# A strided convolution with group norm and GELU, forward and backward, on one core: 1 MB gradient stores move to GpSimd's queue, GELU's cube term becomes two instructions, two spreading copies replace three, and the order tables are written anew

## Chip, cores and metric

The kernel runs on 1 core of one Trainium2 chip. The metric is device time in microseconds (us); less is better. The time before is the median of three runs. The profile is that of one further execution.

## What is computed

```python
# x [2,16000,256], w [31,256,256], gamma, beta [256], grad_out [2,7985,256], all bf16
h = sum over i of einsum('blc,cd->bld', x[:, i:i+2*L:2, :], w[i])     # K=31, stride 2, L=7985
mu, var = mean and variance of h over l, per batch and channel
out = gelu_tanh((h - mu) / sqrt(var + 1e-5) * gamma + beta)
# returned: out, and the gradients of x, w, gamma, beta for grad_out
```

So there are three large matrix products: the convolution (forward), the gradient of `x`, and the gradient of `w`.

## The kernel before, in words

The three products are not done tap by tap. Taps are grouped by the branches A, B_ and C_, and a Karatsuba-like scheme at up to three levels replaces products by sums and differences of operands: VectorE (DVE) prepares the sums in SBUF (all large tiles are pieces of one buffer `arena`), TensorE (PE) multiplies into PSUM (`ps`, four slots of two banks in `ring`), ScalarE (ACT) and DVE combine results there.

The work has five stages, named in the code by `plan.stage`:

- **F0**, **F1**: the forward convolution of batch 0 and of batch 1. `f_sums` (L688 to L730, helper line L694) makes operand sums on DVE, `f_mm` (L736) multiplies, `f_three_b` (L756) multiplies one shared product into the first bank and then spreads it, with signs, over both banks by ACT copies (L772). In F1 the GELU of batch 0 and its derivative run beside it (`gelu_batch`, `gelu_unit`, L1086).
- **G0**, **G1**: the gradient of `x`. `input_grad` (L1411) goes over batch `b`, chunk `c` (four of them), half `pr` and branch. `e_load` (L1191) brings two spilled tensors back from DRAM (`dyd`, `hd`, 512 KB each for each `dh`), `e_comp` (L1199) combines them on DVE (L1206, L1208, L1217) and ACT spreads the result. `g_sums` (L1277) makes differences, `g_mm` (L1324) multiplies, `g_evac` (L1387) adds a PSUM pair to `GRB` into `HO`, a single buffer of 1 MB (L1395), and the fourth such addition of a half is followed by its store to `out_1` (L1399). `dl_turn` (L1254) transposes operand tiles for the next stage by DMA on SyncE's queue (SP, L549) and stores each from GpSimd's queue (POOL) to a DRAM tensor `dld` (128 KB each, 144 of them). In G0 the GELU of batch 1 runs beside it.
- **W**: the gradient of `w`, nine combinations `n` (COMBOS). `x_raw` and `d_tile` load operands on SP, `w_add` (L1496), `pair_x` (L1598), `pair_d` (L1609, L1614) and `leaf_d` (L1699) make sums on DVE, `w_mm` (L1528) multiplies, `w_pairs` (L1617) makes a shared product and spreads it by ACT copies (L1630), `w_both` (L1638), `ve` (L816) and `keep` (L831) move partial results, `w_emit` (L1550, L1557) writes finished taps and stores them.

**What sets the order.** Every operation is recorded by `Plan.add` with an engine, an estimated duration and its data. `Plan.order` gives each a due time, worked back from the position of PE's work, and shifts it by two tables in us: `lead`, by stage and function, and `fine`, by stage, function and part (chunk or `n`). `Plan.listing` then makes a list of each engine's instructions from the estimated durations and due times, and `emit` issues them in that order, which is kept. So every engine runs its instructions strictly in the listed order: an instruction that waits holds up all that stand behind it on its engine. The estimated duration of an ACT instruction of `n` elements comes from `act(n)` (L31).

`load` (L536) sends a transfer of over 4096 bytes to SP in every stage, whatever queue its caller names, unless `own=True` is passed. So the stores of `out_1` go through SP, in one row with the loads of `e_load`, the transposes and the loads of stage W; the `dld` stores pass `own=True` and go through POOL.

Of the kernel before, what the change touches and what calls it, by code (L numbers as in the profile page):

```python
# [12 lines left out]
ACT = mybir.ActivationFunctionType  # L13
# [17 lines left out]
def act(n, extra=0.0):  # L31
    return 0.06 + n * 0.00097 + extra
# [6 lines left out]
class Plan:  # L39
# [3 lines left out]
    def __init__(self, tc):  # L43
# [10 lines left out]
            "F0 f_evac last": 5.0,  # L54
            "F0 f_mm f_leaf": -288.0,
            "F0 f_mm f_outer": -149.5,
            "F0 f_mm f_three_ac": -4.5,
            "F0 f_mm f_three_b": -5.5,
            "F0 f_mm pe_turn": -527.0,
            "F0 f_outer forward": -46.0,  # L60
            "F0 f_seed forward": -48.5,
            "F0 f_three_b forward": -129.5,
            "F0 keep f_evac": 35.5,
            "F0 load conv_stem_kernel": -15.5,
            "F0 load f_evac": 42.5,
            "F0 tt f_sums": -120.5,
            "F0 tt second": 20.5,
            "F0 tt third": -36.0,
            "F0 turn w2_part": -3.0,
            "F0 turn x_load": -8.5,  # L70
            "F0 ve f_seed": -122.5,
            "F0 ve_neg f_seed": 49.0,
            "F0 w_sub f_first": -76.5,
            "F0 w_sum w2_part": -13.5,
            "F1 f_evac last": -106.5,
            "F1 f_mm f_leaf": -335.0,
            "F1 f_mm f_outer": 74.0,
            "F1 f_mm f_three_ac": -8.5,
            "F1 f_mm f_three_b": -75.5,
            "F1 f_three_b forward": -73.0,  # L80
            "F1 gelu_unit gelu_batch": -2.0,
            "F1 load gelu_unit": 23.0,
            "F1 load out0_store": 15.0,
            "F1 tt f_sums": -79.5,
            "F1 tt gelu_unit": -49.5,
            "F1 tt second": -38.0,
            "F1 tt third": -225.5,
            "F1 turn gelu_batch": 56.0,
            "F1 turn gelu_unit": -12.5,
            "F1 turn x_load": 35.5,  # L90
            "F1 w_sub f_again": 4.5,
            "G0 e_comp e_load": 0.5,
            "G0 g_evac last": 1.5,
            "G0 g_mm g_leaf": -24.5,
            "G0 g_mm g_outer": 22.0,
# [369 lines left out]
def conv_stem_kernel(  # L465
# [620 lines left out]
    def gelu_unit(b, c, e, tiles, go, oo):  # L1086
# [23 lines left out]
        def tt(o, a, b_, op):  # L1110
            add("DVE", dve(nf), [o], [a, b_], lambda: V.tensor_tensor(out=o, in0=a, in1=b_, op=op))  # L1111
# [745 lines left out]
```

## Time and profile before

| what | value |
|---|---|
| median of three runs | 1153.68 us (1152.89 to 1154.54) |
| the profiled execution's own time | 1154.13 us |
| its span, first to last instruction | 1152.4 us |
| mean granted TensorE clock | 0.994 |
| PE, DVE, ACT, POOL busy | 1122.5, 997.9, 532.7, 125.4 us |
| DMA issues of 1 MB (and two of 832 KB) from `arena` to `out_dram` on SP | 14 and 2 |

How to read it: PE is the engine that is nearly always busy, so the profile's useful questions are where PE is idle and what ended each idle stretch. DVE has little room either, but its idle time costs nothing by itself. The view of waits lists, for each engine and line, what was waited for, the total in us, how often, and the longest. The timeline gives the start, the length, the engine and line, and in brackets the idle time of that engine just before, with what ended it. A `q` behind an engine's name means its queue's sequencer: it issues DMAs or waits.

### The profile page before, as it was taken

To read this page: it belongs to the slowest core of one execution; us is meant where nothing else is said; L and a number is where in the kernel's file an instruction comes from. 1 tells how busy PE (TensorE), PEld (TensorE's weight loads), DVE (VectorE), ACT (ScalarE), POOL (GpSimd) and SP (SyncE) were. 2 spreads that over 40 slices of the span, in tenths; PEclk is the share of its full clock that TensorE was granted. 3 is DMA by queue.
4 is the path that set the end of the run, shared out by engine and by line. 5 is a ranking of instruction groups with operands and counts; after the bars stand their busy time and mean duration, and the time that the engine had idled before them with its cause. 6 is when DMAs were issued, how large, how long until landed. Compare 5 with 4: busy or idle time off the path is not lost. (4 is left out here: it accounts for less than half of the span.)

```text
span 1152.4 us, 18848 instructions
## 1 busy us (share of the span) xinstructions
PE 1122.5 (97%) x7652; PEld 749.9 (65%) x7652; DVE 997.9 (87%) x920; ACT 532.7 (46%) x817; POOL 125.4 (11%) x221
## 2 busy tenths in 40 slices
PE   5999999999999999999999899999999999999998
PEld 3888899877777874444444344444588666656785
DVE  7997787798989997999999787877799998689995
ACT  1354444768776588897744355722211212211200
POOL 0000000000000012232323223232100000000000
PEclk8999999999999999999999999999999999999999
DMA  9476657769795599999888779787997825899484
GB/s 219 69 189 119 167 156 150 171 173 203 189 232 129 203 370 267 278 274 270 225 213 189 154 203 214 201 218 147 297 293 225 305 88 167 303 296 371 146 254 119
DMA packets 345807, 243.57 MB, mean 211 GB/s; under 512 B 233377, under 2 KB 316967, under 8 KB 341543
## 3 DMA queue, kind: packets, MB, share of 16 engines
q1 hardware_dynamic: 338615, 223.47, 72.5%
q0 software_dynamic: 7104, 18.89, 5.9%
q8 instruction: 60, 0.98, 0.4%
q14 instruction: 28, 0.23, 0.1%
HBM read 106.24 MB, written 80.25 MB: 162 GB/s over the span
## 5 line engine op out<-in xcount | busy, mean ns | idle before, releaser
L736 PE MATMUL ps<-arena 128*128 128x256 bf16 (+4 forms) x3460 | 407.8, 281 | 12.4 <-DMA arena<-in_x_dram 5.5
L1324 PE MATMUL ps<-arena 128*128 128x512 bf16 x1872 | 404.5, 377 | 6.9 <-DVE arena L1277 3.4
L736 PEld LDWEIGHTS <-arena 128*128 128x128 bf16 x3460 | 338.9, 99 | 81.0 <-DMA arena<-in_x_dram 5.7
L1324 PEld LDWEIGHTS <-arena 128*128 128x128 bf16 x1872 | 183.5, 98 | 226.8 <-issue 11.4
L1528 PE MATMUL ps<-arena 128*128 128x256 bf16 (+1 forms) x2320 | 311.2, 297 | 6.5 <-DVE arena L1598 4.9
L1528 PEld LDWEIGHTS <-arena 128*128 128x128 bf16 x2320 | 227.5, 98 | 90.3 <-DVE arena L1598 5.7
L831 ACT ACTIVATE arena<-ps 128x1024 f32<-128x1024 f32 x109 | 111.0, 1022 | 262.3 <-PE ps L1528 90.1
L694 DVE TENSOR_TENSOR arena<-arena 128x2080 bf16<-128x2080 bf16 (+8 forms) x126 | 156.5, 1267 | 34.0 <-PE ps L736 33.6
L544 POOL DMA_DIRECT2D dld<-arena x144 | 104.3, 727 | 261.9 <-DMA arena<-arena 248.3
L1111 DVE TENSOR_TENSOR arena<-arena 128x2048 bf16<-128x2048 bf16 (+1 forms) x80 | 95.7, 1196 | 9.6 <-ACT arena L1103 5.3
L1277 DVE TENSOR_TENSOR arena<-arena 128x1032 bf16<-128x1032 bf16 (+1 forms) x126 | 87.5, 725 | 8.7 <-ACT arena L1226 3.3
L1496 DVE TENSOR_TENSOR arena<-arena 128x4096 bf16<-128x4096 bf16 x38 | 86.2, 2286 | 7.4 <-DMA arena<-in_x_dram 3.8
L1385 DVE TENSOR_TENSOR ps<-ps,arena 128x2048 f32<-128x2048 f32 x30 | 68.9, 2296 | 26.0 <-ACT arena L831 14.8
L1395 DVE TENSOR_TENSOR arena<-ps,arena 128x1024 bf16<-128x1024 f32 x64 | 77.0, 1218 | 8.1 <-PE ps L1324 4.8
L851 ACT ACTIVATE arena<-ps 128x512 bf16<-128x512 f32 (+1 forms) x64 | 37.1, 581 | 54.0 <-PE ps L736 53.4
L1630 ACT COPY ps<-ps 128x256 f32<-128x256 f32 x54 | 19.2, 358 | 85.2 <-PE ps L1528 84.1
L553 POOL MEMSET arena<- 128x128 bf16 (+11 forms) x40 | 8.6, 245 | 425.4 <-DVE arena L694 140.0
L1351 ACT COPY ps<-ps 128x512 f32<-128x512 f32 x48 | 27.7, 578 | 46.8 <-PE ps L1324 45.6
L1699 DVE TENSOR_TENSOR arena<-arena 128x4608 bf16<-128x4608 bf16 x16 | 40.6, 2551 | 4.7 <-PE ps L1528 4.7
L806 ACT ACTIVATE arena<-ps 128x512 f32<-128x512 f32 x56 | 29.7, 597 | 32.5 <-DVE ps L816 18.8
L772 ACT ACTIVATE ps<-ps 128x256 f32<-128x256 f32 x75 | 27.6, 369 | 34.7 <-PE ps L736 33.5
L1614 DVE TENSOR_TENSOR arena<-arena 128x2048 bf16<-128x2048 bf16 x36 | 42.8, 1218 | 0.8 <-DMA out_dram<-arena 0.8
(81 smaller groups left out, 717.1 us busy)
## 6 DMA issues: line engine op xcount, KB each, us to landing
arena<-in_x_dram SPq DMA_DIRECT2D x40, 1024.0 KB
dld<-arena POOLq DMA_DIRECT2D x144, 128.0 KB, 3.9
arena<-hd SPq DMA_DIRECT2D x32, 512.0 KB
out_dram<-arena SPq DMA_DIRECT2D x14, 1024.0 KB
arena<-dld SPq DMA_DIRECT2D x18, 640.0 KB
arena<-dld SPq DMA_DIRECT2D x18, 576.0 KB
vl<-arena SPq DMA_DIRECT2D x36, 256.0 KB
arena<-vl SPq DMA_DIRECT2D x9, 1024.0 KB
```

What stands on the lines that cost most here:

```text
L544: lambda: e.dma_start(out=out, in_=in_), dma=np_ * ns / 16e3 * 1.03, ns=ns, tp=SH[pk], slack=slack)
L694: lambda: nc.vector.tensor_tensor(out=o, in0=a, in1=b, op=ALU.add))
L736: yield nc.tensor.matmul(ps[:, dh, cs], lhsT=wt, rhs=mv, start=s0, stop=False, skip_group_check=True)
L831: lambda: nc.scalar.activation(out=out, in_=ps, func=ACT.Copy, scale=scale))
L1111: add("DVE", dve(nf), [o], [a, b_], lambda: V.tensor_tensor(out=o, in0=a, in1=b_, op=op))
L1277: lambda: nc.vector.tensor_tensor(out=o, in0=a, in1=b, op=ALU.subtract))
L1324: yield nc.tensor.matmul(ps[:, e, 0:wide], lhsT=lt, rhs=mv, start=s0, stop=False, skip_group_check=True)
L1385: lambda: nc.vector.tensor_tensor(out=o, in0=x, in1=g, op=ALU.add))
L1395: lambda: nc.vector.tensor_tensor(out=ho[:, :, k, :], in0=ps[:], in1=g, op=ALU.add))
L1496: add("DVE", dve(4096), [o], [a, b], lambda: nc.vector.tensor_tensor(out=o, in0=a, in1=b, op=ALU.add))
L1528: yield nc.tensor.matmul(ps[:, s, c0:c1], lhsT=lt, rhs=mv, start=s0, stop=False, skip_group_check=True)
L1614: add("DVE", dve(2048), [o], [u, v], lambda o=o, u=u, v=v: nc.vector.tensor_tensor(out=o, in0=u, in1=v, op=ALU.subtract))
```

## The change

Five edits.

1. The store of a finished half of `out_1` passes `own=True`, so GpSimd issues it. These 16 transfers leave SP's row and stand in POOL's, among the `dld` stores.
2. In `gelu_unit`, `z = (y2 + 1/a) * y` was one scalar_tensor_tensor; it becomes a tensor_scalar (add) and a tensor_tensor (multiply), with `z` rounded to bf16 between them.
3. In `f_three_b` and `w_pairs` three ACT copies of 256 elements become one of 256 and one of 512 (the second writes two pieces by a stepped or repeated view).
4. `act(n)` is another line: 0.15 + 0.00085 n in place of 0.06 + 0.00097 n.
5. Both tables of shifts hold other numbers and partly other keys, so the lists of all engines differ from before in many places. No matrix product is added or removed.

```diff
 def act(n, extra=0.0):
-    return 0.06 + n * 0.00097 + extra
+    return 0.15 + n * 0.00085 + extra
...
-            "G1 load e_load": -8.0,
+            "G1 load e_load": -10.5,
...
-            "G1 load e_load": {0: -112.0, 1: -15.0, 2: -56.0, 3: 1.0},
+            "G1 load e_load": {0: -88.5, 1: 40.5, 3: -2.0},
...
-        for o, i, sc in ((ps[:, 1, 0:HM], ps[:, 0, HM:512], 1.0), (ps[:, 1, HM:512], ps[:, 0, HM:512], -1.0),
-                         (ps[:, 0, HM:512], ps[:, 0, 0:HM], -1.0)):
-            add("ACT", act(256), [o], [i],
+        for o, i, sc in ((ps[:, 1, 0:HM], ps[:, 0, HM:512], 1.0), (ps[:, :, HM:512], ps[:, :, 0:HM], -1.0)):
+            add("ACT", act(o.free_size()), [o], [i],
...
-        add("DVE", dve(nf, 1), [z], [y2, y],
-            lambda: V.scalar_tensor_tensor(out=z, in0=y2, scalar=1.0 / GELU_A, in1=y, op0=ALU.add, op1=ALU.mult))
+        add("DVE", dve(nf, 4), [z], [y2],
+            lambda: V.tensor_scalar(out=z, in0=y2, scalar1=1.0 / GELU_A, scalar2=None, op0=ALU.add))
+        tt(z, z, y, ALU.mult)
...
-                 ho[0:r].rearrange("p e k f -> p (e k f)"), r * 8192, 4096, "POOL", slack=60.0)
+                 ho[0:r].rearrange("p e k f -> p (e k f)"), r * 8192, 4096, "POOL", slack=60.0, own=True)
...
-            for o, i in ((ps[:, 1, 0:D], ps[:, 0, D:512]), (ps[:, 1, D:512], ps[:, 0, D:512]), (ps[:, 0, D:512], ps[:, 0, 0:D])):
-                add("ACT", act(256), [o], [i], lambda o=o, i=i: nc.scalar.copy(out=o, in_=i))
+            v = ps[:, 0, D:512]
+            v = bass.AP(tensor=v.tensor, offset=v.offset, ap=[list(v.ap[0]), [0, 2], [1, D]])
+            for o, i in ((ps[:, 1].rearrange("p (q d) -> p q d", q=2), v), (ps[:, 0, D:512], ps[:, 0, 0:D])):
+                add("ACT", act(o.free_size()), [o], [i], lambda o=o, i=i: nc.scalar.copy(out=o, in_=i))
```

What the new tables and the new queue do to the order is seen at three places. Line numbers of the changed kernel are 2 or 3 lower than those of before in most functions.

**SP, early in G1** (batch 1, from the loads of chunk 0 to those of chunk 1; `hd_1` and `dyd_1` are chunk 1's loads, two pairs, one for each `dh`; `x8` counts a row's repeats). Before:

```order
L549 DMA_TRANSPOSE arena<-arena 128x4x128 x6
L544 DMA out_dram<-arena 128x4096
L549 DMA_TRANSPOSE arena<-arena 128x4x128 x6
L544 DMA out_dram<-arena 104x4096
L544 DMA arena<-dyd_1_73 128x2048
L544 DMA arena<-hd_1_65 128x2048
L549 DMA_TRANSPOSE arena<-arena 128x4x128 x8
L544 DMA arena<-dyd_1_73 128x2048
L544 DMA arena<-hd_1_65 128x2048
```

The same stretch of the changed kernel:

```order
L547 DMA_TRANSPOSE arena<-arena 128x4x128 x6
L542 DMA arena<-hd_1_65 128x2048
L547 DMA_TRANSPOSE arena<-arena 128x4x128
L542 DMA arena<-dyd_1_73 128x2048
L547 DMA_TRANSPOSE arena<-arena 128x4x128 x4
L542 DMA arena<-hd_1_65 128x2048
L547 DMA_TRANSPOSE arena<-arena 128x4x128 x3
L542 DMA arena<-dyd_1_73 128x2048
```

The stores are gone from the row. Of the first pair, the load of `hd_1` now stands nine transposes further forward than before and that of `dyd_1` eight; the second pair has also moved forward, in between the transposes that stood ahead of it.

**DVE, where combination 0 of stage W ends and 1 begins** (L1699 is `leaf_d`, L1496 `w_add`, L1598 `pair_x`, L1614 `pair_d` or a half of it, L1638 `w_both`). Before:

```order
L1614 TENSOR_TENSOR arena<-arena 128x2048 x2
L1638 TENSOR_TENSOR ps<-ps,arena 128x1024
L1699 TENSOR_TENSOR arena<-arena 128x4608 x2
L1496 TENSOR_TENSOR arena<-arena 128x4096 x2
L1598 TENSOR_TENSOR arena<-arena 128x2048 x2
```

The same place of the changed kernel, where L1494, L1596 and L1612 are the lines L1496, L1598 and L1614 of before:

```order
L1612 TENSOR_TENSOR arena<-arena 128x2048 x2
L1638 TENSOR_TENSOR ps<-ps,arena 128x1024 x3
L1596 TENSOR_TENSOR arena<-arena 128x2048
L1494 TENSOR_TENSOR arena<-arena 128x4096 x2
L1596 TENSOR_TENSOR arena<-arena 128x2048 x2
L1699 TENSOR_TENSOR arena<-arena 128x4608 x2
```

The two `leaf_d` went from ahead of the two `w_add` and two `pair_x` to behind them, and one other `pair_x` came ahead.

**DVE, where combination 4 of stage W ends and 5 begins.** Before:

```order
L1598 TENSOR_TENSOR arena<-arena 128x2048
L1496 TENSOR_TENSOR arena<-arena 128x4096 x3
L1598 TENSOR_TENSOR arena<-arena 128x2048
L1614 TENSOR_TENSOR arena<-arena 128x2048
L1699 TENSOR_TENSOR arena<-arena 128x4608
```

The same place of the changed kernel:

```order
L1596 TENSOR_TENSOR arena<-arena 128x2048
L1494 TENSOR_TENSOR arena<-arena 128x4096 x3
L1612 TENSOR_TENSOR arena<-arena 128x2048
L1596 TENSOR_TENSOR arena<-arena 128x2048
L1699 TENSOR_TENSOR arena<-arena 128x4608
```

Here a `pair_d` (L1612) now stands ahead of the second `pair_x` (L1596).

On POOL, each store of `out_1` now stands between two pairs of `dld` stores, each of which waits there for its transpose. At the very end, PE's list before closes with single products for halves of a slot, so the last `w_emit` is one of 256 elements with one store; in the changed kernel PE closes with two `w_leaf` groups, and the last `w_emit` is one of 1024 elements with two stores.

More of the change, by code (lines that the diff above doesn't have):

```diff
@@ L66, in __init__ @@
[L66 to L92, printed above, removed]
@@ L134, in __init__ @@
[L134 to L139 removed]
+            "F0 f_evac last": -16.5,
+            "F0 f_mm f_outer": -267.0,
+            "F0 f_mm f_three_ac": -22.5,
+            "F0 f_mm f_three_b": -38.5,
+            "F0 f_mm pe_turn": -374.5,
+            "F0 f_outer forward": -61.5,
+            "F0 f_seed forward": 49.5,
```

338 lines of the change are left out of this document (178 added, 160 removed).

## The prediction, made before the changed kernel ran

> **What bounds the kernel now.** I read the page's sums first, then busy time by stretches, then PE's own waits, then the timeline round each wait of PE over 0.5 us.
>
> ```profile
> span 1152.4 us, 18848 instructions
> PE 1122.5 (97%) x7652; PEld 749.9 (65%) x7652; DVE 997.9 (87%) x920; ACT 532.7 (46%) x817; POOL 125.4 (11%) x221
> ...
> 0.00:25.00 25.00, 12.97 (x84) 8.77 (x85) 18.59 (x22) 3.94 (x6) 2.39 (x14) 0.90 1.02 246
> ...
> 600.00:700.00 100.00, 96.46 (x440) 43.19 (x438) 84.81 (x87) 44.66 (x59) 28.38 (x47) 0.98 0.80 184
> 800.00:900.00 100.00, 95.87 (x733) 71.28 (x732) 90.56 (x66) 24.28 (x33) 7.24 (x10) 1.00 0.92 258
> 1000.00:1100.00 100.00, 97.20 (x688) 67.70 (x686) 89.61 (x62) 16.81 (x29) 0.00 (x0) 0.98 0.84 281
> ```
>
> PE is the bound: busy 1122.5 of 1152.4 us. The change adds and removes no product, so those 1122.5 us stay and only PE's 29.9 us of idle time can move. In the stretches the first number behind the comma is PE's busy time: 25.00 - 12.97 = 12.0 us idle at the start, 3.5 in 600 to 700, 4.1 in 800 to 900, 2.8 in 1000 to 1100; with 4.1 behind PE's last product (rows of C) that is 26.5 of the 29.9. DVE, the third number, is 85 to 91% busy in these stretches, yet PE seldom stands still for it, so an instruction saved on DVE or ACT is worth only what PE waits for it.
>
> ```profile
> PE ps L1528 <- DVE arena L1598: 4.9, 3, 2.8
> ...
> PE ps L1324 <- DVE arena L1277: 3.4, 1, 3.4
> ...
> PE ps L1324 <- DVE arena L1395: 0.9, 1, 0.9
> PE ps L1528 <- DVE arena L1609: 0.6, 1, 0.6
> ```
>
> At the start DVE's list, up to the weight differences that PE waits for there, holds the same instructions before and after, two pairs of them swapped, so I leave its 12.0 us as they are. What can go is 3.4 behind L1277, 4.9 behind L1598 in three pieces, 0.6 behind L1609.
>
> **The change part by part.** A, *the store of `out_1` off SP* (early G1):
>
> ```profile
> SPq L544 <- DVE arena L1395: 23.4, 9, 5.5
> ...
> 643.65 0.50 SPq L544 DMA_DIRECT2D out_dram<-arena  x1
> 644.20 0.35 SPq L544 DMA_DIRECT2D arena<-dyd  x1
> 644.59 1.81 SPq L544 DMA_DIRECT2D arena<-hd  x1
> 646.99 15.89 SPq L549 DMA_TRANSPOSE arena<-arena  x8
> 653.17 0.75 DVE L1208 TENSOR_SCALAR arena<-arena,stats 128x2048 bf16<-128x2048 bf16 x1 [1.48 <-DMA arena<-dyd]
> 655.81 0.81 DVE L1206 TENSOR_SCALAR arena<-arena,stats 128x2048 bf16<-128x2048 bf16 x1 [1.88 <-DMA arena<-hd]
> 658.40 1.22 DVE L1395 TENSOR_TENSOR arena<-ps,arena 128x1024 bf16<-128x1024 f32 x1
> 658.54 3.78 PE L1324 MATMUL ps<-arena 128*128 128x512 bf16 x9 [3.39 <-DVE arena L1277]
> ```
>
> SP stood still for 23.4 us behind evacuations (L1395), mostly for these stores. Here the store goes out at 643.65, the two loads of chunk 1 stand right behind it and share the DMA engines with its 832 KB, and DVE waits 1.48 + 1.88 = 3.36 us for them. The difference that PE needs (L1277) is queued behind, and PE stands for 3.39. In the changed order the loads are 8 and 9 transposes further forward and no store is ahead. A transposing issue on SP takes 15.89 / 8 = 2.0 us here, waits included, so they go out some 16 us earlier, far over the 3.36 missing. **A = -3.4**; bounds -3.4 and 0 (0 if the loads must wait for their buffers instead). What is late next is the g_seed or evacuation behind it on DVE, which waits for PE, not the reverse.
>
> POOL pays for A. Its issue of a store stands among `dld` issues of 726 ns:
>
> ```profile
> L544 POOL DMA_DIRECT2D dld<-arena x144: 726/726/773, 448.5 to 826.8; - x144
> ...
> DMA to landing us min/median/max: 2.2/3.9/9.7
> ...
> 657.51 1.45 POOL L544 DMA_DIRECT2D dld<-arena  x2 [10.58 <-DMA arena<-arena]
> ```
>
> 16 x 0.73 = 11.7 us more on an engine that is 11% busy: nothing on the path by itself. The store adds a wait to POOL, for the fourth evacuation of a half. Queued behind it there are `dld` stores, whose buffers the transposes on SP need again, and small edge copies, which the L1277 of the next chunk need. I take 0, since POOL already waits up to 10.58 us at a time for transposes in these rows and PE did not stand still for POOL; the price if it goes wrong is R2.
>
> The Trainium skill (SBUF — State Buffer, section SBUF: two separate sides) says that a DMA from GpSimd's queue starves for descriptors while DVE runs a one-source instruction that takes both its ports, and advises SP or ACT; it speaks against this edit. By this rule each store could be held for one such DVE instruction, at most the 0.81 us of L1206, 16 x 0.81 = 13 us on POOL and none on PE. The row does not show it: 144 issues last 726 to 773 ns beside a DVE that is 85% busy in 600 to 700, so the sum holds nothing for it.
>
> B, *`leaf_d` behind `pair_x`* (W, combination 0 to 1):
>
> ```profile
> 837.10 1.36 DVE L1694 TENSOR_TENSOR arena<-arena 128x2304 bf16<-128x2304 bf16 x1 [0.66 <-DMA arena<-dld]
> ...
> 855.66 5.02 DVE L1699 TENSOR_TENSOR arena<-arena 128x4608 bf16<-128x4608 bf16 x2
> 860.59 4.49 DVE L1496 TENSOR_TENSOR arena<-arena 128x4096 bf16<-128x4096 bf16 x2
> 864.99 2.35 DVE L1598 TENSOR_TENSOR arena<-arena 128x2048 bf16<-128x2048 bf16 x2
> 866.27 0.61 PE L1528 MATMUL ps<-arena 128*128 128x256 bf16 x4 [1.57 <-DVE arena L1598]
> ```
>
> DVE runs without a gap; PE waits for the two L1598 (1.57, and 4.9 - 1.57 - 2.80 = 0.53 for the second). The changed order puts the 5.02 us of L1699 behind them and one L1598 (1.2) ahead: they come 3.8 us earlier, over the 2.10 missing. DVE had no wait ahead of L1496, so its operands were there by 860.59, perhaps only just. What is late next is L1699, which the next products but one need. **B = -2.1**, bounds -2.1 and 0. In the same block the 0.6 for L1609 has DVE held 0.66 at L1694 just ahead, by a load of `dld`; in the changed lists that load is ahead of combination 1's, and the L1609 ahead of the L1694: **B' = -0.6**, bounds -0.6 and, if the load is later, +0.6.
>
> C, *the end*:
>
> ```profile
> 1146.76 1.58 PE L1528 MATMUL ps<-arena 128*128 128x256 bf16 x13
> 1147.51 1.56 DVE L1557 TENSOR_TENSOR arena<-ps,arena 128x1024 bf16<-128x1024 f32 x2 [1.32 <-PE ps L1528]
> 1148.76 1.42 SPq L544 DMA_DIRECT2D out_dram<-arena  x3
> ```
>
> PE ends at 1148.34, SP's last issue at 1150.18, 1.84 later. Before, only the last part of 1.56 us of additions and one issue followed PE. Now an addition of 1024 elements (1.22, as the L1395 among the rows of A) and two issues of 1.42 / 3 = 0.47 do: 1.22 + 0.94 and some 0.1 for the handover, 2.26. **C = +0.4**; bounds 0 and +1.0 (if one more issue's time goes into the landing).
>
> D, *`pair_d` ahead of the second `pair_x`* (W, 4 to 5):
>
> ```profile
> 1003.54 4.62 DVE L1496 TENSOR_TENSOR arena<-arena 128x4096 bf16<-128x4096 bf16 x2 [3.23 <-DMA arena<-dld]
> 1008.19 1.23 DVE L1598 TENSOR_TENSOR arena<-arena 128x2048 bf16<-128x2048 bf16 x1
> 1009.34 1.22 DVE L1614 TENSOR_TENSOR arena<-arena 128x2048 bf16<-128x2048 bf16 x1
> 1009.48 2.81 PE L1528 MATMUL ps<-arena 128*128 128x256 bf16 x15 [2.80 <-DVE arena L1598]
> ```
>
> PE waits 2.80 for L1598, which now stands behind the L1614: 1009.34 - 1008.19 = 1.15 later. The 3.23 us that DVE waits ahead may shrink or grow, since one `dld` load moved ahead of two loads of `x`. **D = +1.1**; bounds -2.8 (all of the wait gone) and +2.4 (the 1.15 and as much again from that load).
>
> E, *the copies and the gelu*:
>
> ```profile
> L1101 DVE SCALAR_TENSOR_TENSOR arena<-arena 128x2048 bf16<-128x2048 bf16 x12 | 27.5, 2288 | 5.4 <-ACT arena L1098 5.2
> L1107 DVE TENSOR_SCALAR arena<-arena 128x2048 bf16<-128x2048 bf16 x12 | 8.3, 688 | 0.1
> L1111 DVE TENSOR_TENSOR arena<-arena 128x2048 bf16<-128x2048 bf16 x60 | 73.3, 1221 | 7.8 <-ACT arena L1103 4.4 <-ACT arena L1105 2.7
> L1630 ACT COPY ps<-ps 128x256 f32<-128x256 f32 x54 | 19.2, 358 | 85.2 <-PE ps L1528 84.1
> L1351 ACT COPY ps<-ps 128x512 f32<-128x512 f32 x48 | 27.7, 578 | 46.8 <-PE ps L1324 45.6
> 834.82 3.65 PE L1528 MATMUL ps<-arena 128*128 128x256 bf16 x32 [0.35 <-ACT ps L1630]
> ```
>
> Gelu: 688 + 1221 = 1909 ns for 2288, so 0.38 us less, 16 times: 6.1 us of DVE. PE's other work hides all of it, since no wait of PE names the gelu's lines; if DVE's list fell behind there it would be worth up to the 0.9 that PE waits for L1395. Copies: 358 + 578 = 936 ns for 3 x 358 = 1074, so 0.14 less, in 54 / 3 = 18 places in W and in each `f_three_b`; PE waits for one of them (0.35). **E = -0.15**, bounds -1.25 (that 0.9 and all of the 0.35) and 0. The new line for `act` costs nothing but the order.
>
> **Sum**: -3.4 - 2.1 - 0.6 + 0.4 + 1.1 - 0.15 = -4.75. The profiled execution took 1154.13, 1.73 more than its span; that rest stays, so 1149.4. It is 0.45 over the median of the three runs (1153.68), from which the sum gives 1148.9. I say 1149.0.
>
> **The rivals.** *R1: the loads don't gain, A stays.* The stretch 600 to 700 has PE idle for 3.5 us; if the loads of chunk 1 wait for the one buffer that the previous `dh` still holds, an earlier place in SP's row is empty. For it: the second pair went out only after the first had been combined (two pairs for one buffer). Against it: DVE combined the previous pair long before 643. The time is 1149.0 + 3.4 = 1152.4. The Trainium skill (DMA: Bandwidth & Descriptors, section Issuing engines are not separate DMA queues) says that issuing from another engine saves only the sequencer's time, because all transfers share 16 engines; by it the gain must come from SP's standing still, and this rival is what is left where it doesn't.
>
> *R2: GpSimd issues the store late, slower than before.* `HO` is a single buffer. In the rows of A the store goes out at 643.65, as soon as its data is there, and the next half overwrites `HO` at 658.40: 14.75 us. With the longest landing seen on POOL, 9.7 us, 5 us are spare. A store now stands behind two `dld` issues that wait for transposes, up to 10.58 us. If one is 10.6 late, L1395 waits 10.6 - 5 = 5.6 us, and everything behind it on DVE, then PE. It decides from 5 us of lateness. Two of 16 stores so would cost some 11 us, less 2 for PE's lead: +9, 1158. Against it: transposes also lose their wait behind the stores on SP, so they land earlier.
>
> *R3: more goes than I count.* With 6 us less on DVE and D's wait gone (-2.8 in place of +1.1), -3.9 more: 1145.
>
> *R4: the new order opens waits of its own* as long as those that it closes (A + B + B' = 6.1): 1155. Most of the lists are new and each of PE's 29 us is a place where an order failed on the chip.
>
> **How the numbers follow.** My forecast .50, R1 .14, R2 .08, R3 .14, R4 .14. About 0.2%, 2.3 us, is what a measurement of this kernel can tell from no change (the three runs lie within 1.65 us): faster is below 1151.4, slower above 1156.0. Faster: .46 of the forecast's .50, all of R3, .02 of R1: .62. Slower: all of R2, .08 of R4's .14 (two waits more), .02 of the forecast's: .18. The same: the rest, .20. The range runs from 1145 (R3) to 1157 (R4 and the mild end of R2); it leaves out R2 at its price and the far ends of R3 and R4, some .15.
>
> **What would show it.** A: no wait of PE for L1277 of over 1 us in 600 to 700, and SP's waits for L1395 gone from its list. B: no wait for `pair_x` (L1596 there) at the change to combination 1. C: about 4.5 us from PE's last product to the end. D: a wait of about 3.9 us at the change to 5. E: DVE near 992 us busy. R2: DVE's evacuation waiting for a store, POOL issuing stores over 5 us after their data. I am wrong if PE's idle time outside the start doesn't fall by 3 to 6 us, and wrong in the ground if PE's busy time itself changes.

## The result, and the profile after

The changed kernel is **slower by 0.6%**: median 1162.47 us of 14 runs (1155.81 to 1168.31) against 1154.12 us of 14 runs of the kernel before (1151.81 to 1160.89); the ratio is 1.0061, 95% interval 1.0043 to 1.0079 (it is not the quotient of the two medians, which lie 0.7% apart). The profiled execution took 1163.37 us, 1.77 more than its span.

The page's sums and the stretches of the changed kernel, in the columns of the tables of before (PE's busy time is the first number behind the comma, DVE's the third; the granted clock is the third number from the end, full speed is 1.00):

```profile
span 1161.6 us, 18833 instructions
PE 1121.7 (97%) x7652; PEld 748.6 (64%) x7652; DVE 993.2 (85%) x936; ACT 526.2 (45%) x774; POOL 140.2 (12%) x237
```

```profile
0.00:25.00 25.00, 12.42 (x81) 8.31 (x82) 17.97 (x21) 3.93 (x6) 2.37 (x14) 0.92 0.99 242
...
400.00:500.00 100.00, 96.58 (x561) 54.64 (x559) 86.10 (x108) 79.18 (x118) 21.61 (x34) 1.00 1.01 292
500.00:600.00 100.00, 94.30 (x435) 42.74 (x434) 88.36 (x101) 75.02 (x86) 31.50 (x53) 0.98 0.99 244
600.00:700.00 100.00, 96.87 (x448) 43.51 (x447) 91.53 (x105) 49.02 (x65) 35.00 (x54) 1.00 0.83 201
...
800.00:900.00 100.00, 93.99 (x684) 66.35 (x683) 83.22 (x61) 22.14 (x28) 10.51 (x15) 1.00 0.98 260
...
1000.00:1100.00 100.00, 96.74 (x659) 64.21 (x658) 90.14 (x59) 17.66 (x24) 0.00 (x0) 1.00 0.84 277
```

PE's busy time is what it was (1121.7 for 1122.5), as foreseen; its idle time went from 29.9 to 1161.6 - 1121.7 = 39.9 us. DVE lost 4.7 us (6.1 were foreseen for the gelu), and PE gained nothing from it. PE's own waits say where:

```profile
PE ps L1526 <- DVE arena L1596: 7.1, 5, 3.3
...
PE ps L1322 <- DVE arena L1393: 4.7, 2, 4.2
...
PE ps L1322 <- DVE ps L1383: 2.4, 3, 1.4
...
PE ps L734 <- ACT ps L769: 1.6, 1, 1.6
```

L1596 is `pair_x`, L1393 the evacuation into `HO`, L1383 `g_seed`, L769 the spread of a shared product in the forward stage. By place, in us of PE's waiting (its waits over 0.15 us), with a second profiled execution of the changed kernel (the run `a_again` below, span 1155.8):

| place (us in the changed kernel) | before | changed | changed, again |
|---|---|---|---|
| start, to 25 | 12.0 | 12.6 | 12.7 |
| 406, end of F1 | 0 | 1.6 | 2.3 |
| 450 to 535, G0 | 2.7 | 3.2 | 3.7 |
| 590 | 0 | 4.2 | 0.6 |
| 611 to 624, into G1 | 0 | 2.9 | 2.9 |
| the loads of chunk 1 (658 in before) | 3.4 | 0 | 0 |
| 803 to 808 | 0 | 0.7 | 0.7 |
| opening of W, 827 to 910 | 4.0 | 5.8 | 4.6 |
| change to combination 5 (1009 in before) | 2.8 | 3.3 | 2.3 |

The wait of term A is gone. Four places that had no wait in before have one now (406, 590, 611 to 624, 803 to 808), and at three more the waits differ by less; a table further down takes all of them over more executions. The length of the one at 590 belongs to one execution: DVE stood 3.49 us for a transpose that had landed late, and the next execution has 0.6 there.

```profile
585.12 1.23 DVE L1275 TENSOR_TENSOR arena<-arena 128x2064 bf16<-128x2064 bf16 x1 [3.49 <-DMA arena<-arena]
...
590.29 24.52 PE L1322 MATMUL ps<-arena 128*128 128x512 bf16 x104 [4.20 <-DVE arena L1393]
```

The others come again. Into G1 and at the opening of W:

```profile
615.77 1.90 PE L1322 MATMUL ps<-arena 128*128 128x512 bf16 x8 [0.96 <-DVE arena L1275]
...
619.11 4.26 PE L1322 MATMUL ps<-arena 128*128 128x512 bf16 x20 [1.44 <-DVE ps L1383]
...
623.91 2.37 PE L1322 MATMUL ps<-arena 128*128 128x512 bf16 x9 [0.54 <-DVE arena L1393]
```

```profile
836.29 4.61 DVE L1393 TENSOR_TENSOR arena<-ps,arena 128x1024 bf16<-128x1024 f32 x4
...
838.13 1.91 PE L1526 MATMUL ps<-arena 128*128 128x256 bf16 x16
840.82 3.48 DVE L1596 TENSOR_TENSOR arena<-arena 128x2048 bf16<-128x2048 bf16 x3
842.09 1.92 PE L1526 MATMUL ps<-arena 128*128 128x256 bf16 x16 [2.05 <-DVE arena L1596]
844.22 2.49 DVE L1607 TENSOR_TENSOR arena<-arena 128x1024 bf16<-128x1024 bf16 x4
844.96 10.65 PE L1526 MATMUL ps<-arena 128*128 128x256 bf16 x96 [0.95 <-DVE arena L1607]
...
854.00 1.23 DVE L1612 TENSOR_TENSOR arena<-arena 128x2048 bf16<-128x2048 bf16 x1 [2.21 <-DMA out_dram<-arena]
855.14 2.35 DVE L1596 TENSOR_TENSOR arena<-arena 128x2048 bf16<-128x2048 bf16 x2
856.42 0.61 PE L1526 MATMUL ps<-arena 128*128 128x256 bf16 x4 [0.80 <-DVE arena L1596]
```

Here DVE does four evacuations in one go (4.61 us), and the `pair_x` for PE's next product stands behind them. The same place in before:

```profile
827.22 3.48 DVE L1395 TENSOR_TENSOR arena<-ps,arena 128x1024 bf16<-128x1024 f32 x3
827.36 1.89 PE L1324 MATMUL ps<-arena 128*128 128x512 bf16 x8 [0.35 <-DVE ps L1385]
...
829.09 1.91 PE L1528 MATMUL ps<-arena 128*128 128x256 bf16 x16
830.61 1.22 DVE L1598 TENSOR_TENSOR arena<-arena 128x2048 bf16<-128x2048 bf16 x1
...
830.83 1.89 PE L1324 MATMUL ps<-arena 128*128 128x512 bf16 x8
831.74 1.29 DVE L1609 TENSOR_TENSOR arena<-arena 128x1024 bf16<-128x1024 bf16 x2
...
832.56 1.91 PE L1528 MATMUL ps<-arena 128*128 128x256 bf16 x16
832.95 1.22 DVE L1395 TENSOR_TENSOR arena<-ps,arena 128x1024 bf16<-128x1024 f32 x1
```

There PE did 8 products of G1, then 16 of W, 8 of G1 and 16 of W, and DVE did three evacuations, a `pair_x` and two `pair_d` before the fourth. In the changed list all products of G1 come first, so nothing is left for PE to do while DVE catches up. In the second execution the 2.05 is there again, but the clock falls behind it (PE takes 2.71 us in place of 1.92 for the next 16 products), and of the 0.95 only 0.17 is left. At 854.00 DVE waits 2.21 us for the last store of `out_1`, whose buffer `HO` stage W uses again; with every store on SP (`a_lists_sp` below) it waits 3.27 us there, so this wait is not GpSimd's.

### The profile page after: what moved, and what is told of

Same layout as the page of the kernel before. It is cut to its first block, busy times and chain, and to the rows that moved or that the text cites. A ratio compares the mean times of both kernels' runs of the same rounds, so it can differ in the third digit from the quotient of the medians.

```text
span 1161.6 us, 18833 instructions
## 1 busy us (share of the span) xinstructions
PE 1121.7 (97%) x7652; PEld 748.6 (64%) x7652; DVE 993.2 (85%) x936; ACT 526.2 (45%) x774; POOL 140.2 (12%) x237
## 4 chain that ended last, share of the span: by engine, by line
PE 74%; DVE 13%; DMA 6%; ACT 2%; issue 2%; SPq 2%; DVEq 0%; ACTq 0%
PE ps L734 31%; PE ps L1322 25%; PE ps L1526 18%; DVE arena L1494 2%; DMA arena<-in_x_dram 1%; DVE ps L1383 1%; SPq L542 1%; DMA out_dram<-arena 1%; DMA arena<-arena 1%; DVE arena L1098 1%; DVE arena L1393 1%; DVE ps L1638 1%; DVE arena L1596 1%; DMA arena<-hd 1%; ACT arena L828 1%
## 5 line engine op out<-in xcount | busy, mean ns | idle before, releaser
L1322 PE MATMUL ps<-arena 128*128 128x512 bf16 (+1 forms) x1872 | 404.8, 377 | 11.8 <-DVE arena L1393 4.7
L1098 DVE TENSOR_TENSOR arena<-arena 128x2048 bf16<-128x2048 bf16 (+1 forms) x96 | 114.8, 1195 | 10.1 <-ACT arena L1105 5.2
L1383 DVE TENSOR_TENSOR ps<-ps,arena 128x2048 f32<-128x2048 f32 x30 | 68.9, 2298 | 28.1 <-PE ps L1322 15.0
L1494 DVE TENSOR_TENSOR arena<-arena 128x4096 bf16<-128x4096 bf16 x38 | 86.2, 2285 | 7.5 <-DMA arena<-in_x_dram 7.3
L1393 DVE TENSOR_TENSOR arena<-ps,arena 128x1024 bf16<-128x1024 f32 x64 | 76.6, 1218 | 14.0 <-PE ps L1322 14.0
L1630 ACT COPY ps<-ps 128x512 f32<-128x512 f32 (+1 forms) x36 | 16.6, 465 | 91.8 <-PE ps L1526 79.9
L542 POOL DMA_DIRECT2D out_dram<-arena x20 | 11.7, 588 | 342.5 <-DMA arena<-yd 286.2
L1612 DVE TENSOR_TENSOR arena<-arena 128x2048 bf16<-128x2048 bf16 x36 | 42.8, 1218 | 2.4 <-DMA out_dram<-arena 2.2
L1699 DVE TENSOR_TENSOR arena<-arena 128x4608 bf16<-128x4608 bf16 x16 | 40.7, 2551 | 2.3 <-PE ps L1526 2.3
```

Of the source, the lines that this page charges most:

```text
L542: lambda: e.dma_start(out=out, in_=in_), dma=np_ * ns / 16e3 * 1.03, ns=ns, tp=SH[pk], slack=slack)
L1322: yield nc.tensor.matmul(ps[:, e, 0:wide], lhsT=lt, rhs=mv, start=s0, stop=False, skip_group_check=True)
L1383: lambda: nc.vector.tensor_tensor(out=o, in0=x, in1=g, op=ALU.add))
L1393: lambda: nc.vector.tensor_tensor(out=ho[:, :, k, :], in0=ps[:], in1=g, op=ALU.add))
L1494: add("DVE", dve(4096), [o], [a, b], lambda: nc.vector.tensor_tensor(out=o, in0=a, in1=b, op=ALU.add))
L1612: add("DVE", dve(2048), [o], [u, v], lambda o=o, u=u, v=v: nc.vector.tensor_tensor(out=o, in0=u, in1=v, op=ALU.subtract))
```

## The experiments

Theory 1: the lists of the change cost the time, by waits that they open. Theory 2: the stores on GpSimd's queue cost it. Theory 3: one of the edits on DVE or ACT does. Since the planner makes other lists whenever a recorded operation changes, "before's lists" below means the order of before, kept, with only what is issued at a place changed. The letters A to E are the prediction's. Ratios are to before, with 95% intervals; 0.1% is 1.15 us. Some traces hold the records of 7598 products instead of 7652; there I use waits and not PE's sum.

### Code and lists apart

`b_lists_a_code`: before's lists with the three code edits. (The second, merged copy of `f_three_b` stands at the third's place, where a product may already have added to a bank, so part of the outputs is changed.)

```diff
-            lambda: e.dma_start(out=out, in_=in_), ...
+            lambda: (q or e).dma_start(out=out, in_=in_), ...      # q = GpSimd for out_1
-            lambda: V.scalar_tensor_tensor(out=z, in0=y2, ..., in1=y, ...))
+            lambda: both V.tensor_scalar and V.tensor_tensor, in its place
```

> The lists of before on every engine, with all three code edits put in where their old instructions stood: stores of out_1 issued by GpSimd, z by two instructions, two copies. Theory 1 (the new order of the lists costs the time, the code edits don't): 0 to -1 us against before, ratio 0.998 to 1.001. Theory 2 (the store on GpSimd's queue costs it, since its packets share the DMA engines with the transposes on SP's queue): +5 to +8 us, ratio 1.004 to 1.007. Theory 3 (one of the DVE or ACT edits costs it): +5 to +8 us as well, to be told from 2 by the kernel that moves the store alone.

1.0052 (1.0027 to 1.0077). Theory 1 alone falls: these edits cost in before's lists too. The longest new wait of PE is 6.91 us, at the change to combination 1.

`b_lists_pool`: only the first line of that diff.

> Before with its lists, only the 16 stores of out_1 issued by GpSimd. Prediction's term A: -3.4 us, ratio 0.997. Theory 1: within 1 us of before. Theory 2: +5 to +8 us.

**1.0069** (1.0046 to 1.0091), so the cost is the stores'. The wait at 658 is gone (0.22), and waits of 1.72 at 671 and 0.88 at 710 are new; at the change to combination 1 PE waits 4.05 + 0.47 in place of 1.57 + 0.53.

`a_lists_sp`: the changed kernel, its 16 stores issued by SP at the same point of the order.

> The changed kernel, only the 16 stores of out_1 issued by SP instead of GpSimd at the same point of the order. Theory 1 (order): +5 to +8 us against before, as the change. Theory 2 (store's queue): 0 to +2 us. If SP standing still for evacuations matters as the prediction said, slower than the change by some 3 us: ratio 1.009.

**1.0055** (1.0034 to 1.0076). Theory 2 alone falls as well: without any store on GpSimd the changed lists cost as much. The waits of the changed kernel are there again: 1.99 at 407, 0.96 + 1.44 + 0.54 at 613 to 621, 0.72 at 805, 2.06 + 0.95 at 839 to 842.

`a_lists_b_code` was meant as the fourth corner.

> The lists of the change on every engine, with the old code at the same places: the store issued by SP at the point of the order where the change has it on GpSimd, z by one instruction, three copies. Theory 1 (order): still +5 to +9 us, ratio 1.004 to 1.008, with PE waits in G0 and at W's changes of combination as after the change. Theory 2 or 3 (code): 0 to +2 us, ratio 1.000 to 1.002.

1.1149 (1.1121 to 1.1178), which says nothing on the question. One replaced record had another name and so lost its entry in the tables, and the lists came out different in all of G0, G1 and W (and `z` is formed where `y` isn't always written yet). It shows only how much the tables carry: with one name missing the kernel takes 131 us more.

### One store among sixteen

In `b_lists_pool` the longest new wait lies behind the last store. SP's transpose of `yd` is in flight there; in before's row the store stood behind it. `b_last_pool` puts only this store on GpSimd, `b_all_but_last_pool` the other 15.

```diff
+                 q=nc.gpsimd if b == NB - 1 and c == NCK - 1 and pr == 1 else None)   # or: if not (...)
```

> Before with its lists and only the last of the 16 stores of out_1 (832 KB, the one in the opening of W) issued by GpSimd. Theory 1 (this store now goes out while SP's transpose of yd is in flight, shares the DMA engines with it, and holds SP and the loads of combination 1 behind it): the issue of that transpose lasts 19 to 23 us on SP instead of 13.3, PE's wait for pair_x at the change to combination 1 is 4 to 7 us instead of 2.1, the time +3 to +5 us, ratio 1.003 to 1.004. Rival (all 16 stores cost a little each): transpose and wait as before, +0.4 us. At 658 us, where SP issues as in before: a wait of PE of 3.4 us if the wait that term A took away belongs to the order; none if it was a stall of one execution.

> Before with its lists and 15 stores of out_1 issued by GpSimd, the last one by SP. Theory 1: the opening of W as in before (transpose of yd 13 us, wait for pair_x about 2.1), time +2 to +4 us against before, that is some 3 to 4 less than with all 16. Rival (each store costs a little): +7 us.

**1.0045** (1.0023 to 1.0067) and 1.0013 (0.9995 to 1.0030). One of 16 stores has most of the cost. In `b_last_pool`:

```profile
832.83 18.17 SPq L549 DMA_TRANSPOSE arena<-yd  x1
...
839.05 0.59 POOL L544 DMA_DIRECT2D out_dram<-arena  x1 [6.76 <-DVE arena L1395]
...
862.23 5.03 DVE L1699 TENSOR_TENSOR arena<-arena 128x4608 bf16<-128x4608 bf16 x2 [1.89 <-DMA arena<-dld]
...
872.85 7.37 PE L1528 MATMUL ps<-arena 128*128 128x256 bf16 x38 [2.85 <-DVE arena L1598]
```

The issue of the transpose holds SP for 18.17 us, 13.27 in before (12.89 in `b_all_but_last_pool`), so all that follows on SP goes out some 5 us later; `leaf_d` waits for its `dld` load, `pair_x` stands behind it, PE waits. (Expected were 19 to 23 us for the transpose, and 4 to 7 us of waiting.) PE's waits from 840 to 873 are only 1.5 us longer than in before (4.85 for 3.32). Most of the rest is in the stretch behind the wait:

```profile
865.00:870.00 5.00, 4.99 (x46) 4.22 (x44) 5.00 (x3) 1.84 (x2) 0.00 (x0) 1.00 1.12 324
870.00:875.00 5.00, 2.05 (x9) 1.16 (x10) 5.00 (x5) 1.02 (x1) 0.00 (x0) 0.70 1.06 211
875.00:880.00 5.00, 5.00 (x31) 3.75 (x29) 5.00 (x5) 1.44 (x5) 0.00 (x0) 0.62 0.74 207
880.00:885.00 5.00, 5.00 (x48) 4.49 (x47) 5.00 (x5) 0.70 (x2) 0.00 (x0) 1.00 0.75 219
```

The granted clock falls: 31 products in 875 to 880 where 48 follow in the next 5 us. A mean of 5 us mixes full and half speed and takes in the wait; in stretches of 2 us from PE's restart at 872.85 the clock is 0.50, 0.50, 0.51 and 1.00. That is 1.00 + 1.00 + 0.98 = 3.0 us lost, and 1.5 + 3.0 = 4.5 of the 5.2 measured. (This execution is among the longer of its kernel, and 2.2 us of its waits more than before's lie in G0, ahead of the store.) Behind before's 1.57 + 0.53 the clock stays at 1.00. The Trainium skill (TensorE: Matmul & The Clock Gate, section Why this matters for your kernels, the row on throughput drops in the middle of a kernel) says that an idle gap of over about 3 us sends PE back to half speed. The half speed agrees with this trace; the 3 us don't, since the clock falls here behind 2.85 us, and also behind a wait of 2.15 at 526 and one of 1.97 at 1018.

Is it GpSimd's queue, or that the store runs beside the transpose? `b_last_act` issues it from ACT's queue (`q=nc.scalar`); `b_last_pool_late` leaves it on GpSimd, behind a small copy that reads what the transpose wrote.

> Before with its lists and only the last store of out_1 issued by ScalarE's queue, at the same point of the order as the kernel that had it on GpSimd. Theory 1a (what costs is that the store runs beside SP's transpose of yd instead of behind it, on whatever queue): as that kernel, the transpose's issue 18 to 23 us on SP, PE's wait for pair_x at the change to combination 1 about 2.9 to 4, ratio 1.003 to 1.005. Theory 1b (it is GpSimd's own queue): transpose about 13 us, ratio 1.000.

> Before with its lists and only the last store of out_1 issued by GpSimd, but behind a copy on GpSimd that reads what the transpose of yd wrote, so that the store cannot go out before this transpose has landed. Theory 1a: the transpose's issue is back at 13 us and the loads of combination 1 are not late, PE's wait for pair_x 2.1 as before, time within 1.5 us of before; against that only the later free buffer HO (DVE waits 0.83 us for this store before; up to 3 now). Theory 1b: +3 to +5 us still.

1.0038 (1.0016 to 1.0060): from ACT too the transpose takes longer, 15.75 us, PE waits 2.75, and the clock falls to 0.50. So it is the company that costs, whatever the queue. Whether GpSimd's queue lengthens the transpose further (18.17 us for 15.75, one execution of each) stays open; the two ratios can't be told apart. The Trainium skill (DMA: Bandwidth & Descriptors, section Issuing engines are not separate DMA queues) says that transfers of all issuers run on the same 16 engines and interleave; the 15.75 and 18.17 us of the transpose beside the store, for 13.27 ahead of it, agree.

1.0027 (1.0008 to 1.0046) for the late store. Its transpose is back at 13.16 us and the loads of combination 1 are in time, but `HO` comes free late, and that is dearer than I expected:

```profile
828.39 13.16 SPq L553 DMA_TRANSPOSE arena<-yd  x1
...
857.04 2.36 DVE L1618 TENSOR_TENSOR arena<-arena 128x2048 bf16<-128x2048 bf16 x2 [5.80 <-DMA out_dram<-arena]
...
858.32 4.00 PE L1532 MATMUL ps<-arena 128*128 128x256 bf16 x18 [4.50 <-DVE arena L1618]
```

So the store has a narrow place: earlier it holds SP, later it holds `HO`. SP's row, where it goes out right behind the transpose, was the best of the places tried.

### The copies and the gelu alone (term E)

`b_gelu_copies`: before's lists and stores, the two other code edits (here with every copy where it belongs).

> Before with its lists and stores on SP, only z by two instructions and the shared products spread by two copies. Prediction's term E: -0.15 us (-1.25 to 0), DVE near 992 us busy, no wait of PE that names the gelu's lines. If one of these edits costs: over +2 us. At 658 us the same question as above, since nothing there differs from before.

1.0005 (0.9991 to 1.0019); DVE is 992.1 us busy. Theory 3 falls; term E's -0.15 us is too small to be seen, and nothing speaks against it.

### The moved `leaf_d` alone (term B)

`b_leaf_moved`: before with two instructions of DVE moved; `b_best` moves them past both `pair_d` too and has the edits of term E.

```diff
-  leaf_d x2, w_add x2, pair_x x2, pair_d x2
+  w_add x2, pair_x x2, leaf_d x2, pair_d x2      (b_leaf_moved)
+  w_add x2, pair_x x2, pair_d x2, leaf_d x2      (b_best)
```

> Before with one thing in its order changed: at combination 1 the two leaf_d on DVE stand behind the two pair_x instead of ahead of the sums for them. Prediction's term B: PE's waits for pair_x there (1.57 + 0.53) gone, time -2.1 us, ratio 0.998. Rival: the sums or pair_d that are next on DVE are late in their place, the time within 1 us of before.

> Before with its lists and stores on SP, z by two instructions and two copies, and at combination 1 the two leaf_d on DVE behind both the pair_x and the pair_d. If the wait of 2.84 us that came in the place of the one removed belongs to the pair_d behind the leaf_d: both waits gone, PE waits under 0.5 us there, time -2 us, ratio 0.998. Rival: the leaf_d are then late for their own product, ratio 1.000 or above.

**1.0019** (1.0003 to 1.0034) and **1.0024** (1.0007 to 1.0041): both slower than before, if only just, though the wait they aim at is gone in both (0.24 and none). In the first, the `pair_d` is late instead:

```profile
864.66 5.02 DVE L1710 TENSOR_TENSOR arena<-arena 128x4608 bf16<-128x4608 bf16 x2
...
869.60 2.35 DVE L1625 TENSOR_TENSOR arena<-arena 128x2048 bf16<-128x2048 bf16 x2
...
870.87 9.31 PE L1539 MATMUL ps<-arena 128*128 128x256 bf16 x69 [2.84 <-DVE arena L1625]
```

0.24 + 2.84 for 2.10 is 1.0 more, and behind the 2.84 the clock is 0.50 and 0.67 in two stretches of 2 us, 1.7 lost: 2.7 us in all, 2.2 measured (0.3 to 3.9). In the second the wait comes back later, in smaller pieces, 3.95 us to 902:

```profile
876.65 7.16 PE L1547 MATMUL ps<-arena 128*128 128x256 bf16 x64 [1.46 <-DVE arena L1613]
884.53 3.65 PE L1547 MATMUL ps<-arena 128*128 128x256 bf16 x32 [0.72 <-DMA arena<-in_x_dram]
889.00 1.25 PE L1547 MATMUL ps<-arena 128*128 128x256 bf16 x10 [0.81 <-DVE ps L1667]
```

One row of before's stretches says why another order of DVE did not help here:

```profile
860.00:900.00 40.00, 37.90 (x346) 33.49 (x345) 40.00 (x28) 10.86 (x15) 0.00 (x0) 1.00 0.76 218
```

DVE, the third number, is busy for all 40.00 us. I read PE's 2.1 us of waiting as what DVE's work is too long by: both other orders only chose another product to wait.

### The lists of the change at the opening of W

`a_pairs_first`: the changed kernel with DVE's order altered there.

```diff
-  evacuation x4, pair_x x3, pair_d x2
+  evacuation x2, pair_x, evacuation x2, pair_d x2, pair_x x2
```

> The changed kernel with DVE's order altered in one place, the opening of W: the pair_x for the second half of the first product stands ahead of the last two evacuations of out_1, and the two pair_x that nothing needs yet stand behind the first two pair_d. If the new lists themselves cost time there (PE waits 2.05 + 0.95 behind four evacuations in a row): these waits fall from 3.0 to about 0.7, time -2.3 us against the change, ratio 1.004 against before. Rival: the evacuations now free PSUM late, and PE waits for them instead: 1.006 as the change.

1.0075 (1.0047 to 1.0104). The waits fell from 3.0 to 1.2 (0.90 and 0.28), as expected of the first theory, and the time did not follow, since the next wait grew from 0.80 to 4.28:

```profile
837.55 7.60 PE L1537 MATMUL ps<-arena 128*128 128x256 bf16 x68 [0.90 <-DVE arena L1618]
...
850.50 1.23 DVE L1623 TENSOR_TENSOR arena<-arena 128x2048 bf16<-128x2048 bf16 x1 [3.86 <-DMA out_dram<-arena]
...
852.92 19.34 PE L1537 MATMUL ps<-arena 128*128 128x256 bf16 x151 [4.28 <-DVE arena L1607]
```

DVE does not arrive earlier at the buffer `HO`: it starts to wait for the store 43.6 us behind PE's restart at 803.05, as in the changed kernel (restart at 808.19). But the store, now behind the moved evacuations, goes out 1.1 us later by the same measure (837.19 here, 841.20 there) and holds DVE 1.6 us longer. PE waits again the 1.8 us that it had saved, and these 1.6: 0.80 + 1.8 + 1.6 = 4.2. So the order and the store limit this place together, which is why neither alone shows its price there.

`a_last_sp` took the last store by itself in the changed lists. What ran is the reverse of what the expectation says: the last store on SP and the other 15 on GpSimd.

> The changed kernel with 15 stores of out_1 on SP and only the last on GpSimd. Against the changed kernel with all on SP (+5.5 us on before) this adds the last store alone. If the lists are what costs in the changed kernel: +5 to +7 us against before, with PE waits of about 2.05 + 0.95 at the opening of W as in both. If the last store costs in these lists what it costs in before's (4.5): +10 us.

1.0064 (1.0038 to 1.0089), the waits 2.05 + 0.95 again. With all, 15 or none of the stores on GpSimd the changed lists cost 0.51 to 0.64%; the transpose of `yd` holds SP for 10.4 and 10.5 us with the last store on SP and for 12.5 to 16.3 with it on GpSimd, and in these lists this difference does not reach the time.

Taken together, the changed lists ran in five profiled executions (the changed kernel twice, `a_lists_sp`, `a_pairs_first`, `a_last_sp`). Beside them stand those executions of before's lists in which neither the order at the place nor a store ahead of it was altered (four of them have the edits of term E). Sums of PE's waits over 0.15 us:

| place (us) | before's lists (executions) | changed lists (5) | difference of the means |
|---|---|---|---|
| end of F1, 398 to 425 | 0 to 0.6 (10) | 1.6 to 2.6 | +2.0 |
| G0, 450 to 540 | 2.5 to 4.9 (10) | 2.7 to 3.7 | -0.3 |
| 580 to 605 | 0 (10) | 0.8 to 0.9, once 4.2 | +1.5 |
| into G1, 605 to 632 | 0 to 0.3 (10) | 2.9 to 3.1 | +2.9 |
| the loads of chunk 1, 650 to 668 | 3.2 to 3.4 (7) | 0 | -3.3 |
| 798 to 815 | 0 (10) | 0.7 | +0.7 |
| opening of W, 815 to 912 | 3.5 to 4.5 (5) | 4.6 to 5.8 | +1.6 |
| change to combination 5, 1000 to 1030 | 1.7 to 2.8 (7) | 2.3 to 3.7 | +0.8 |
| behind PE's last product | 4.0 (7) | 4.5 to 4.6 | +0.6 |

The sum is +6.5 us, where these kernels measured 0.51 to 0.75% more, 5.9 to 8.7 us: the waits that the lists open, less the one that they close, account for the cost. G0 has no part in it: before's own lists wait there between 2.5 and 4.9 us from one execution to the next.

### The loads of chunk 1 without GpSimd (term A)

`b_loads_first`: before, SP issues the two loads ahead of the store. `b_loads_first2`: also the next pair one transpose further forward, and the edits of term E.

```diff
-  store out_1, load dyd, load hd, transpose x8, load dyd, load hd
+  load dyd, load hd, store out_1, transpose x8, load dyd, load hd                (b_loads_first)
+  load dyd, load hd, store out_1, transpose x7, load dyd, load hd, transpose     (b_loads_first2)
```

> Before with one thing in SP's order changed: at 643 us the two loads of chunk 1 stand ahead of the store of out_1 instead of behind it; the store stays on SP. Term A: PE's wait of 3.4 us for L1277 at 658 gone, time -3.4 us, ratio 0.997. Rival (given back): the wait gone, waits of 1.7 and 0.9 to 1.4 us for L1395 at 671 and 711 in its place, time within 1 us of before. Second rival (loads don't gain, R1): the wait stays.

> As the kernel with the loads of chunk 1 first, and with the next pair of loads one transpose further forward, z by two instructions and two copies; stores on SP. If what gives the gain back at 671 us is the next pair of loads, landing late behind SP's transposes: that wait falls from 1.7 to under 0.5, time -2 to -3 us against before, ratio 0.997 to 0.998. Rival: it comes back at 711 or in the opening of W, ratio 1.000.

0.9988 (0.9968 to 1.0007) and **0.9964** (0.9946 to 0.9982). The wait at 658 is gone in both. (It belongs to the order and not to one execution: the six other runs that leave this part of SP's row as it was have 3.22 to 3.38 there.) In the first, the next pair is late:

```profile
668.48 0.76 DVE L1218 TENSOR_SCALAR arena<-arena,stats 128x2048 bf16<-128x2048 bf16 x1 [2.31 <-DMA arena<-dyd]
...
670.41 3.83 PE L1334 MATMUL ps<-arena 128*128 128x512 bf16 x17 [2.06 <-DVE arena L1405]
```

3.39 became 2.06, and the clock stays at 1.00 behind it, where before's 3.39 was followed by 0.81 from 660 to 665. In the second the wait is still 1.72. Since it was the best of many, it ran again, beside the changed kernel:

> The same kernel as before in this series (loads first, next pair one transpose further forward, z by two instructions, two copies), a second time. If its gain is real: ratio 0.995 to 0.998 again, no wait of PE at 658 us and one of about 1.7 us at 672. If it was the luck of the best of many: 0.998 to 1.001.

> The changed kernel as it is, a second time, beside the others on one chip. If the waits that its lists open are of the order and not of one execution: about 1.6 to 2.0 us at 406, 1.5 at 531 to 536, 2.9 at 612 to 624, 2.05 + 0.95 at the opening of W again; the 4.2 us at 590, behind a transpose that landed late, was not there with the store on SP and should be gone or much smaller. Ratio 1.004 to 1.008.

0.9984 (0.9967 to 1.0002), with a wait of 0.92 in place of the 1.72: faster by 0.2 to 0.4% over the two, the second interval just touching no change. The changed kernel again: 1.0051 (1.0032 to 1.0070).

## Why the prediction was wrong, point by point

The step that failed before all others: the sum put at nothing what the new lists open. It added up the waits that it saw close (A, B and B', -6.1) and left those that come to R4, with a chance. The changed lists, with every store on SP, cost 0.55%: they open some 10 us of PE's waiting (the table above: 2.0 at the end of F1, 2.9 into G1, 1.5 at 590, 1.6 at the opening of W, and less elsewhere) and close 3.3 at the loads of chunk 1.

- **A, -3.4: the mechanism was right, the net was not.** The wait for L1277 is gone in the changed kernel, and GpSimd isn't needed for it. The step of it that failed is "What is late next is the g_seed or evacuation behind it on DVE, which waits for PE, not the reverse". The next pair of loads is late; of 3.39 us some 2.06 come back within 12 us, and with the stores on GpSimd 1.72 + 0.88. In the changed lists the 2.9 us into G1 stand against it.
- **POOL's cost, 0: not to be told from 0 in the changed kernel (1.0061 and 1.0051 with the stores on GpSimd, 1.0055 without), but by luck: in before's lists the same stores cost 0.69%, in a way that neither this term nor R2 had.** I looked at whom GpSimd's waits would hold and not at what else is in flight when the store goes out. The price is not lateness of the issue: one store, early by the standards of SP's row, runs beside SP's transpose and lengthens it from 13 to 18 us. R2 had the right buffer, `HO`, but the wrong reader: stage W, not the next evacuation (5.80 us in `b_last_pool_late`; in the changed kernel 2.21, less than the 3.27 with every store on SP). The rule of the Trainium skill on descriptors for GpSimd's DMAs, which I cited against the edit, shows in no issue: the 20 from GpSimd to `out_dram` last 567 ns in the median in the changed kernel (510 to 1084). Whether the landings owe it anything was not tried.
- **B, -2.1: the step "What is late next is L1699, which the next products but one need" failed.** `pair_d` was queued behind it. The row of DVE without a gap stood in the prediction; from it followed that less work on DVE, rather than another order, would be needed. Alone, the move costs 2.2 us (0.3 to 3.9). In the changed kernel 0.80 + 0.52 of the 1.57 + 0.53 are left, with 0.79 for `w_both` behind them.
- **B', -0.6: wrong sign.** PE waits 0.95 for L1607, and 2.05 for L1596 ahead of it. I read DVE's list there and not PE's, in which the products of G1 that covered these operations had gone to the front.
- **C, +0.4: right.** From PE's last product (1149.80 + 7.18 = 1156.98) to the end of the span it is 4.6 us, for 4.06: +0.6.

```profile
1149.80 7.18 PE L1526 MATMUL ps<-arena 128*128 128x256 bf16 x33
...
1157.01 1.23 DVE L1555 TENSOR_TENSOR arena<-ps,arena 128x1024 bf16<-128x1024 f32 x1 [1.57 <-PE ps L1526]
```

- **D, +1.1: right in kind, and about half in size.** The wait for `pair_x` is 3.26 (2.32 in the second execution) for 2.80; over the executions of the table its mean rises from 2.1 to 2.6, and all waits at the place by 0.8. One execution says little here: before's own order gives 1.7 to 2.8.
- **E, -0.15: DVE as foreseen**, 992.1 to 993.2 us busy; no gain that can be measured.
- **R4 is what happened**, and I gave it .14 and 1155. I counted what closes (three waits that I could see) and gave what opens a chance instead of a count. The changed lists could be read: in PE's, the products of G1 that move ahead of W's. The waits at 406 and 611 to 624 I did not look for; that the lists open them is shown, by five executions with 1.6 to 2.6 and 2.9 to 3.1 us there, where ten of before's lists have at most 0.6 and 0.3. Which entry of the tables makes them was not tried.
- **The price of a wait.** I took each at its length. Behind waits of 2.75 us and more the clock fell to 0.50 in 18 of 20 cases, worth another 1.4 to 3.1 us; the 0.98 in the rows that I quoted was that. Waits of 1.8 to 2.6 us, which the new lists have many of, sometimes cost clock and sometimes don't: the 2.05 at the opening of W cost no clock in the first execution of the changed kernel and 1.7 us in the second. This widens the spread between executions; it does not make the difference between the kernels, whose mean granted clock is 0.99 or above in nearly every profile of either.

What stays open: in before's lists the stores cost 0.69% and in the changed lists nothing that can be measured, while those lists cost 0.55% without them. Both meet at the opening of W, where `HO`, SP and DVE limit together; why the longer transpose does not reach the time in the changed lists is not shown.

## What to carry to other kernels

A wait that an order removes is worth its length less the next wait behind it: look at the supplying engine's busy time over the next 40 us (at 40.00 of 40.00 two new orders gained nothing), and at the next transfer of the same kind. When a transfer goes to another queue, write down what is in flight at its new moment and who needs its buffer next, for each of its instances: here one of sixteen had most of the cost. When all lists change, count what opens in the bottleneck engine's own new list before counting what closes.

## What the runs showed of the hardware

- In before's lists, the issue of a 1 MB transpose from DRAM takes 12.5 to 13.3 us on SP with the 832 KB store behind it, 15.75 with the store beside it from ACT's queue, and 18.17, 19.48 and 23.32 with the store beside it from GpSimd's. In the changed lists it is 10.4 and 10.5 behind, 12.5, 16.0 and 16.3 beside (GpSimd's).
- PE's granted clock, in all profiles but that of `a_lists_b_code` and behind the first 30 us: it fell to 0.50 behind 18 of 20 waits of 2.75 to 6.91 us (not behind one of 3.26 and one of 3.38), behind 12 of 25 of 1.8 to 2.6 us, and behind one of 16 of 1.56 to 1.78 us. A fall behind the 20 longest cost 1.4 to 3.1 us of work.
- Where a transpose landed late, one execution waited 4.2 us and the next 0.6; the waits in G0 came to 2.5 to 4.9 us in ten executions of the same lists. A wait seen once in a profile is to be looked for in a second one.
